# Casting in DMAs on Pool's queue in a sliding attention with an MLP behind it

## The chip, the cores and the metric

The kernel runs on one core of a Trainium2 chip. The metric is the device time of one execution in microseconds (us). The median of five runs before the change is 326.3 us (325.08 to 328.28).

A core has TensorE (PE, matrix products into PSUM), VectorE (DVE), ScalarE (ACT), GpSimd (Pool) and SyncE (SP). Each works through its own queue of instructions in order and waits for others only by semaphores. SP, ACT and Pool can issue DMA transfers; all of them run on the same 16 DMA engines.

## The reference

There are 8 batches, 8 heads, 576 positions and a head dimension of 64; q, k, v are fp32.

```python
scores = q @ k.T / sqrt(64)
mask_plain = (rel >= 0) & (rel < 32)                        # heads 0..3
mask_dil   = (rel >= 0) & (rel < 128) & (rel % 4 == 0)      # heads 4..7
attn = softmax(where(mask, scores, -1e9))
x = (attn @ v), heads side by side: 4608 tokens x 512
h = x @ w_in                        # 512 x 2048
out = maximum(0.01 * h, h) @ w_out  # 2048 x 512, fp32
```

## The kernel before, in words

Everything is computed on fp16 operands with fp32 sums. A **group** n (0 to 15) is four heads of one batch: n = 2 b for the plain heads and 2 b + 1 for the dilated heads of batch b. A **unit** u = 3 n + s is a third of a group's queries. The MLP goes over 13 chunks of tokens (CHUNKS, L20) for its first product and over 36 blocks of 128 tokens for its second.

The order of all work is written out in one string, PROGRAM (L26 to L72), whose words are issued one after the other (L360 to L396). Each engine's queue is the order of its own instructions in this list; where two words use different engines, their order in the list means little. The words:

- lq:n:p loads q and k of a group, one pair of heads (p = 0 or 1) or both (b). load_qk, L138, on SP. For groups 0 to 4 (n < NPE = 5) a partition holds 9 whole rows; for later groups a transfer has rows of 64 fp32, 256 bytes.
- lv:n loads v (load_v, L155, on SP): plain groups in 96 x 24 rows of 256 bytes, dilated groups in two transfers with rows of 1,024 bytes. Both go to a fp32 staging tile vf.
- lw:i:g loads a quarter of w_in (i = 0) or w_out (i = 1), 1 MB, on SP, into one of three staging tiles (L316).
- cq, cv, cw cast what was loaded to fp16 (L170, L183, L325), on the engine named by a letter: V VectorE, P Pool, A ScalarE. cv also copies v's last 32 partitions of each tile to partitions 0 to 31 of the next, as the window reaches back over a tile's edge.
- B:n:p transposes q and k of one pair on TensorE (pe_transpose, L202, 36 matmuls on 64 x 64), the two copies out of PSUM on the engines named. Groups 5 to 15 are transposed by DMAs instead (T, L197).
- S:u computes the scores of a unit and their exponential on ScalarE (L241). With b the mask is added first by a pair of matmuls from the tile bias; with m it is multiplied in later by M:u on VectorE (L264), from the tile mask.
- D:u sums the exponentials and multiplies with v on TensorE (L273), then takes the reciprocal, either on VectorE (r, one RECIPROCAL) or on ScalarE (l, an Ln and an Exp), and VectorE multiplies into xT, the MLP's input.
- I:c:j is a step of the first MLP product (L334, four matmuls and a ScalarE activation), O:t:g a quarter of a block of the second (L343); the last quarter is followed by a copy and a store on ScalarE's queue.
- Z:n are n filler matmuls on a tile of zeros (wp, L392), mask and band build the mask tiles on Pool (L102).

Two staging tiles hold q, two hold k, one each holds v of the plain and of the dilated heads; transposed q, k and fp16 v exist three times (NB = 3). The first MLP step, I:0:0, stands on TensorE behind 35 fillers, 6 B, 8 S and 6 D steps.

Of the kernel before, what the change touches and what calls it, by code (L numbers as in the profile page):

```python
# [9 lines left out]
FP16 = mybir.dt.float16  # L10
# [4 lines left out]
PAD = 128  # L15
B, H, S, D = 8, 8, 576, 64
DM = H * D
# [4 lines left out]
GRING = 1152  # L22
NEG = -30000.0
# [3 lines left out]
Z:3 lq:1:1 Z:8 lq:0:1 Z:2 cq:0:q:V:1 cq:1:k:A:1 Z:1 lq:0:0 lq:1:0 cq:1:q:P:1 lv:1:b Z:3 cq:0:k:A:1  # L27
B:1:1:VV Z:5 cq:0:q:V:0 Z:1 B:0:1:AA cq:1:k:P:0 Z:2 cq:1:q:V:0 Z:2 S:4:b B:1:0:VA lv:0:b lq:2:b
S:1:b lw:0:0 Z:1 cv:1:V:b cq:0:k:P:0 lq:3:b B:0:0:AA lw:0:1 S:3:b D:4:rp S:0:b D:3:lp cq:2:q:V:b Z:3
S:2:b Z:1 cv:0:P:b lw:0:2 D:0:lp cq:2:k:P:b D:1:l S:5:b B:2:1:AV B:2:0:VA cq:3:k:V:b Z:2 D:2:lp  # L30
cw:0:0:P lw:0:3 lv:2:b Z:1 cq:3:q:P:b S:7:m D:5:l mask S:6:m cw:0:1:V lw:1:0 I:0:0 I:0:1 M:7
B:3:0:AA S:8:m B:3:1:AV I:0:2 I:0:3 S:9:b I:0:4 cw:0:2:V I:0:5 I:0:6 M:6 I:0:7 S:11:m M:8 I:0:8
I:0:9 I:0:10 cw:0:3:V lw:1:1 I:0:11 I:0:12 I:0:13 cv:2:P:b cw:1:0:V I:0:14 I:0:15 cw:1:1:P lw:1:2
I:1:0 I:1:1 I:1:2 I:1:3 I:1:4 cw:1:2:P I:1:5 I:1:6 D:6:lp M:11 D:8:lp D:7:r S:10:m O:0:0 I:1:7 I:1:8
I:1:9 I:1:10 I:1:11 I:1:12 M:10 I:1:13 lv:3:b lw:1:3 O:1:0 O:0:1 O:1:1 cv:3:V:b I:1:14 lq:4:b O:2:0
O:2:1 cq:4:q:P:b cw:1:3:V lv:4:b lq:5:b I:1:15 cq:4:k:P:b O:0:2 D:11:l O:1:2 lq:6:b O:0:3 cq:6:q:P:b
D:10:l O:1:3 O:2:2 B:4:0:AV D:9:l B:4:1:VV S:12:m cq:5:q:V:b cq:5:k:V:b T:5 O:2:3 O:3:0 I:2:0 I:2:1
I:2:2 I:2:3 I:2:4 I:2:5 I:2:6 I:2:7 S:14:m I:2:8 I:2:9 I:2:10 I:2:11 cv:4:A:b cq:6:k:V:b O:3:1
I:2:12 lv:5:b T:6 M:14 O:3:2 I:2:13 M:12 lq:7:b O:3:3 I:2:14 lv:6:b cv:5:P:b I:2:15 I:3:0 I:3:1
I:3:2 O:4:0 I:3:3 I:3:4 S:13:m I:3:5 I:3:6 O:4:1 I:3:7 I:3:8 I:3:9 M:13 I:3:10 I:3:11 I:3:12 I:3:13  # L40
S:15:m D:12:r D:13:lp O:5:0 cq:7:q:P:b M:15 O:4:2 I:3:14 S:16:m M:16 cq:7:k:P:b T:7 lv:7:b lq:8:b
lq:9:b D:14:l O:5:1 O:4:3 S:17:m D:16:lp D:15:l I:3:15 cv:7:P:b M:17 O:5:2 O:6:0 O:6:1 I:4:0 O:5:3
I:4:1 S:19:m O:6:2 O:7:0 O:7:1 O:6:3 O:7:2 I:4:2 I:4:3 D:17:l S:20:m cq:9:k:P:b O:8:0 I:4:4 S:18:m
I:4:5 M:20 O:8:1 I:4:6 O:7:3 O:8:2 S:21:m I:4:7 cv:6:V:b I:4:8 M:18 M:19 D:20:lp S:22:m M:21 D:18:r
I:4:9 I:4:10 O:8:3 I:4:11 I:4:12 I:4:13 M:22 cq:8:k:V:b D:19:lp S:23:m D:22:lp D:21:l I:4:14 I:4:15
O:9:0 O:10:0 I:5:0 O:9:1 O:9:2 cq:8:q:V:b T:8 lv:8:b O:9:3 I:5:1 I:5:2 O:11:0 O:10:1 I:5:3 O:11:1
I:5:4 O:10:2 I:5:5 I:5:6 M:23 O:10:3 cq:9:q:P:b T:9 lq:10:b lq:11:b lv:9:b I:5:7 I:5:8 S:25:m D:23:l
I:5:9 O:11:2 I:5:10 I:5:11 I:5:12 I:5:13 I:5:14 M:25 I:5:15 I:6:0 I:6:1 O:12:0 I:6:2 O:12:1 S:26:m
O:11:3 I:6:3 I:6:4 I:6:5 cv:8:V:b I:6:6 S:28:m O:12:2 O:12:3 S:24:m cq:10:q:P:b I:6:7 I:6:8 I:6:9
O:13:0 cq:11:q:A:b I:6:10 I:6:11 O:13:1 M:28 S:27:m cq:11:k:P:b D:25:r I:6:12 I:6:13 cq:10:k:A:b  # L50
T:10 lv:10:b I:6:14 O:13:2 cv:9:P:b lv:11:b T:11 lq:12:b lq:13:b I:6:15 O:14:0 O:13:3 O:14:1 M:24
O:15:0 D:28:l S:29:m M:27 O:14:2 O:14:3 O:16:0 cq:12:k:P:b O:15:1 D:27:l D:24:lp S:30:m O:16:1
O:15:2 O:15:3 I:7:0 I:7:1 I:7:2 I:7:3 I:7:4 M:29 I:7:5 I:7:6 cv:10:P:b O:16:2 cq:12:q:P:b T:12
lv:12:b lq:15:b M:26 O:16:3 O:17:0 M:30 S:33:m D:29:lp D:26:l cv:11:V:b lv:13:b S:34:m M:33 I:7:7
O:17:1 I:7:8 I:7:9 I:7:10 I:7:11 M:34 I:7:12 I:7:13 I:7:14 D:33:r S:32:m cq:13:q:A:b O:17:2 D:34:lp
S:31:m O:17:3 M:31 I:7:15 O:18:0 O:18:1 D:30:lp D:31:l S:35:m M:35 O:18:2 O:19:0 O:18:3 I:8:0 I:8:1
I:8:2 I:8:3 I:8:4 cq:13:k:P:b T:13 lq:14:b S:38:m I:8:5 I:8:6 I:8:7 I:8:8 I:8:9 O:19:1 I:8:10 I:8:11
I:8:12 O:19:2 I:8:13 I:8:14 I:8:15 M:32 O:20:0 S:36:m M:38 D:35:rp D:32:l S:37:m O:19:3 O:20:1
O:20:2 cv:12:V:b cv:13:P:b M:37 O:21:0 O:20:3 O:22:0 cq:14:q:V:b cq:15:k:A:b M:36 O:21:1 O:22:1
I:9:0 I:9:1 D:38:l S:40:m O:21:2 I:9:2 M:40 O:21:3 I:9:3 cq:15:q:P:b T:15 lv:14:b I:9:4 I:9:5 I:9:6  # L60
D:37:l D:40:rp S:39:m O:22:2 I:9:7 S:41:m D:36:l I:9:8 O:22:3 O:23:0 I:9:9 O:23:1 cq:14:k:P:b T:14
lv:15:b I:9:10 O:23:2 M:39 I:9:11 O:23:3 D:39:l S:47:m I:9:12 I:9:13 I:9:14 I:9:15 M:41 I:10:0
I:10:1 O:24:0 O:24:1 M:47 I:10:2 S:46:m I:10:3 O:24:2 I:10:4 O:25:0 S:45:m cv:15:V:b D:41:l D:47:lp
S:42:m O:25:1 I:10:5 cv:14:V:b O:25:2 I:10:6 M:42 M:46 O:24:3 I:10:7 I:10:8 M:45 I:10:9 S:43:m
D:45:lp D:46:l O:26:0 M:43 I:10:10 O:25:3 I:10:11 I:10:12 S:44:m D:43:r D:42:lp I:10:13 O:26:1
I:10:14 I:10:15 O:26:2 O:26:3 I:11:0 I:11:1 I:11:2 O:27:0 I:11:3 I:11:4 I:11:5 I:11:6 M:44 O:27:1
O:27:2 O:27:3 D:44:lp I:11:7 I:11:8 O:28:0 I:11:9 I:11:10 I:11:11 O:29:0 I:11:12 O:28:1 I:11:13
O:29:1 O:28:2 I:11:14 I:11:15 O:29:2 O:28:3 I:12:0 I:12:1 I:12:2 I:12:3 O:30:0 O:30:1 O:29:3 I:12:4
O:30:2 O:31:0 O:30:3 I:12:5 I:12:6 I:12:7 I:12:8 I:12:9 I:12:10 O:32:0 O:31:1 I:12:11 I:12:12 O:31:2
I:12:13 O:31:3 O:32:1 I:12:14 I:12:15 O:33:0 O:32:2 O:34:0 O:32:3 O:33:1 O:34:1 O:35:0 O:33:2 O:34:2  # L70
O:33:3 O:35:1 O:34:3 O:35:2 O:35:3
# [4 lines left out]
def kernel(ctx: ExitStack, tc: tile.TileContext, q, k, v, w_in, w_out, out):  # L76
# [25 lines left out]
    def band(t, one, other):  # L102
# [7 lines left out]
    band(bias, 0.0, NEG)  # L110
# [5 lines left out]
    NB = 3  # L116
# [6 lines left out]
    vf = [cst.tile([128, 24, D], FP32, name="vf0"), cst.tile([128, 32, D], FP32, name="vf1")]  # L123
    nc.vector.memset(vf[1].rearrange("p (h a r) d -> p h a (r d)", a=2, r=4)[64:128, :, 1, :], 0.0)
    nc.scalar.copy(out=vf[0][0:32].rearrange("p (a t) d -> p a (t d)", a=3),
                   in_=warm[0:32].unsqueeze(1).to_broadcast([32, 3, 512]))
    for t in kT:
        nc.vector.memset(t[:, 0:PAD], 0.0)
        nc.vector.memset(t[:, S:PAD + S], 0.0)
    nc.vector.memset(vf[1][0:32], 0.0)  # L130
# [7 lines left out]
    def load_qk(n, pairs=(0, 1)):  # L138
        b, kind = divmod(n, 2)
        base = (b * H + 4 * kind) * S * D  # L140
        for nm, x in (("q", q), ("k", k)):
            if (n, nm) not in qkf:
                qkf[n, nm] = stg.tile([128, 24, D], FP32, tag=nm + "f", name=nm + "f")
            t = qkf[n, nm]
            if n >= NPE:
                nc.sync.dma_start(t[0:96], rows_ap(x, base, [[D, 96], [96 * D, 24], [1, D]]))
            elif len(pairs) == 2:
                nc.sync.dma_start(t[:, 0:18, :].rearrange("p (a t) d -> p a (t d)", a=2),
                                  rows_ap(x, base, [[9 * D, 128], [2 * S * D, 2], [1, 9 * D]]))
            else:  # L150
                p = pairs[0]
                nc.sync.dma_start(t[:, 9 * p:9 * p + 9, :].rearrange("p t d -> p (t d)"),
                                  rows_ap(x, base + 2 * S * D * p, [[9 * D, 128], [1, 9 * D]]))

    def load_v(n, pairs=(0, 1)):  # L155
        b, kind = divmod(n, 2)
        base = (b * H + 4 * kind) * S * D
        p0, p1 = pairs[0], pairs[-1] + 1
        if kind == 0:
            nc.sync.dma_start(vf[0][32:128, 12 * p0:12 * p1, :],  # L160
                              rows_ap(v, base + 1152 * D * p0, [[D, 96], [96 * D, 12 * (p1 - p0)], [1, D]]))
        else:
            t4 = vf[1].rearrange("p (h a r) d -> p h a (r d)", a=2, r=4)
            for a, i0, w in ((0, 0, 96), (1, 96, 48)):
                nc.sync.dma_start(t4[32:32 + w, 2 * p0:2 * p1, a, :],
                                  rows_ap(v, base + (1152 * p0 + 4 * i0) * D,
                                          [[4 * D, w], [S * D, 2 * (p1 - p0)], [1, 4 * D]]))


    def cast_qk(n, nm, eng, pairs=(0, 1)):  # L170
        if (n, nm) not in qkh:
            qkh[n, nm] = att.tile([128, 24 * D], FP16, tag=nm + "h", name=nm + "h")
        t, f = qkh[n, nm], qkf[n, nm]
        for p in pairs:
# [3 lines left out]
            else:  # L178
                eng(out=t[0:96, 12 * D * p:12 * D * p + 12 * D].rearrange(  # L179
                        "p (t h d) -> p h t d", t=6, h=2),  # L180
                    in_=f[0:96, 12 * p:12 * p + 12, :].rearrange("p (h t) d -> p h t d", h=2))

    def cast_v(n, eng, pairs=(0, 1)):  # L183
        t, f = vh[n % NB], vf[n % 2]
        p0, p1 = pairs[0], pairs[-1] + 1
        if n % 2 == 0:
# [240 lines left out]
```

The softmax here doesn't subtract the row's maximum and nothing guards it: scores larger than these inputs give would overflow.

## Time and profile before

| | |
|---|---|
| median of five runs | 326.3 us |
| profiled execution | 327.01 us, span 325.3 us |
| busy: TensorE / VectorE / ScalarE / Pool | 316.7 / 126.5 / 203.1 / 63.3 us |
| matmuls of the MLP, first and second product | 139.0 and 137.3 us |
| filler matmuls (wp) | 12.2 us |
| weight casts: 5 on VectorE, 3 on Pool | 6.8 and 5.7 us |
| read from / written to HBM | 36.70 / 9.44 MB |

The busy rows are sums over the span; the engines overlap, so they don't add up. The granted TensorE clock is full throughout (0.998 in the mean).

### The profile page before, as it was taken

The page shows a single profiled execution, that of the slowest core. Times are in us where ns is not written, and L with a number is a line of the kernel's source. Part 1 is how long each engine was busy: PE and PEld are TensorE (multiplying, and loading weights), DVE is VectorE, ACT ScalarE, POOL GpSimd, SP SyncE. Part 2 cuts the span into 40 slices and gives each one's busy share as a digit, 9 for nine tenths or more (in the row PEclk, how much of TensorE's full clock was granted, in tenths as well). Part 3 has the DMA queues.
Part 4 walks back from the last instruction along what each step waited for, and adds up shares of the span by engine and source line. Part 5 has one row for each costly group of instructions (what it writes and reads, how often), then busy time and mean ns, then how long its engine had stood idle before and what let it go on. Part 6 is the DMA issues. An engine that isn't in the chain of part 4 may idle for free.

```text
span 325.3 us, 6683 instructions
## 1 busy us (share of the span) xinstructions
PE 316.7 (97%) x2809; PEld 186.4 (57%) x2809; DVE 126.5 (39%) x173; ACT 203.1 (62%) x395; POOL 63.3 (19%) x66
## 2 busy tenths in 40 slices
PE   8979999999999999999999999999999999999995
PEld 2546676566755565565546556655665555555542
DVE  4598538560440783040413482076521670000000
ACT  4479883778765683566837787657764774543412
POOL 3273344025230600024000910062000000000000
PEclk9999999999999999999999999999999999999999
DMA  7999898979969105995099899609610000001012
GB/s 241 270 400 378 287 334 241 289 200 206 213 179 270 54 32 121 253 272 104 3 230 266 193 224 267 144 32 197 164 63 1 34 34 32 32 34 64 4 62 97
DMA packets 111198, 53.06 MB, mean 163 GB/s; under 512 B 96832, under 2 KB 101440, under 8 KB 110656
## 3 DMA queue, kind: packets, MB, share of 16 engines
q1 hardware_dynamic: 105984, 43.20, 53.9%
q10 hardware_dynamic: 5184, 9.44, 7.9%
q8 instruction: 22, 0.36, 0.5%
q14 instruction: 8, 0.07, 0.1%
HBM read 36.70 MB, written 9.44 MB: 142 GB/s over the span
## 4 chain that ended last, share of the span: by engine, by line
PE 93%; DVE 3%; ACT 2%; issue 1%; DVEq 0%
PE op L349 39%; PE hp L339 38%; PE sps L258 5%; PE wp L392 3%; PE den L284 3%; PE o L292 2%; PE tp L209 2%; ACT gt L341 1%; DVE rec L300 1%; DVE vh L195 1%; ACT er L261 0%; ACT ln L297 0%; DVE vh L192 0%; DVE qh L176 0%; ACT rec L298 0%
## 5 line engine op out<-in xcount | busy, mean ns | idle before, releaser
L339 PE MATMUL hp<-xT,w 128*128 128x384 f16 (+1 forms) x832 | 139.0, 315 | 0.7 <-DVE xT L309 0.7
L349 PE MATMUL op<-w,gt 128*128 128x512 f16 x576 | 137.3, 380 | 0.0
L341 ACT ACTIVATE gt<-hp 128x384 f16<-128x384 f32 (+1 forms) x208 | 93.5, 465 | 58.3 <-PE hp L339 56.1
L339 PEld LDWEIGHTS <-w 128*128 128x128 f16 x832 | 89.3, 114 | 43.7 <-DVE xT L309 1.2
L349 PEld LDWEIGHTS <-gt 128*128 128x128 f16 x576 | 54.6, 98 | 57.2 <-issue 0.7
L309 DVE TENSOR_TENSOR xT<-o,rec 128x384 f16<-128x384 f32 (+1 forms) x64 | 33.6, 553 | 95.8 <-ACT rec L298 94.3
L353 ACT COPY ob<-op 128x512 f32<-128x512 f32 x36 | 21.0, 584 | 36.9 <-PE op L349 36.8
L261 ACT ACTIVATE er<-sps 128x768 f16<-128x768 f32 (+1 forms) x48 | 38.6, 804 | 8.7 <-PE sps L258 7.5
L268 DVE TENSOR_TENSOR em<-er,mask 128x768 f16<-128x768 f16 (+1 forms) x41 | 25.2, 637 | 26.4 <-ACT er L261 26.0
L300 DVE RECIPROCAL rec<-den 128x384 f32<-128x384 f32 x9 | 23.0, 2552 | 20.2 <-PE den L284 20.2
L258 PE MATMUL sps<-qT,kT 64*128 64x96 f16 (+1 forms) x448 | 22.9, 229 | 0.6 <-ACT er L261 0.5
L297 ACT ACTIVATE ln<-den 128x384 f32<-128x384 f32 x39 | 18.9, 485 | 5.2 <-PE den L284 3.9
L179 POOL CAST kh<-kf 96x768 f16<-96x768 f32 x12 | 12.8, 1096 | 47.6 <-ACT gt L341 27.7
L258 PEld LDWEIGHTS <-kT 64*128 64x128 f16 (+1 forms) x448 | 15.2, 121 | 11.1 <-issue 9.4
L298 ACT ACTIVATE rec<-ln 128x384 f32<-128x384 f32 x39 | 20.4, 523 | 1.2
L179 POOL CAST qh<-qf 96x768 f16<-96x768 f32 x12 | 11.6, 994 | 36.4 <-DMA out_dram<-ob 26.5
L292 PEld LDWEIGHTS <-vh 128*64 128x64 f16 (+1 forms) x448 | 15.4, 110 | 2.4
L192 POOL CAST vh<-vf 128x2048 f16<-128x2048 f32 x4 | 7.6, 1892 | 41.7 <-PE o L292 25.6
L292 PE MATMUL o<-em,vh 128*64 128x96 f16 (+1 forms) x384 | 14.3, 201 | 0.0
L284 PE MATMUL den<-em,ones 128*64 128x384 f16 (+1 forms) x82 | 14.2, 343 | 0.0
L392 PE MATMUL wp<-xT 128*128 128x512 f16 x35 | 12.2, 458 | 1.7 <-DVE xT L114 1.3
L284 PEld LDWEIGHTS <-ones 128*64 128x64 f16 (+1 forms) x96 | 5.3, 107 | 7.8 <-issue 6.7
(55 smaller groups left out, 130.6 us busy)
## 6 DMA issues: line engine op xcount, KB each, us to landing
out_dram<-ob ACTq DMA_DIRECT2D x36, 256.0 KB, 2.1
qf<-in_q_dram SPq DMA_DIRECT2D x14, 576.0 KB, 7.3
kf<-in_k_dram SPq DMA_DIRECT2D x14, 576.0 KB, 7.2
vf<-in_v_dram SPq DMA_DIRECT2D x8, 576.0 KB, 6.2
wf<-in_moe_w_in_dram SPq DMA_DIRECT2D x4, 1024.0 KB, 11.4
wf<-in_moe_w_out_dram SPq DMA_DIRECT2D x4, 1024.0 KB, 8.8
vf<-in_v_dram SPq DMA_DIRECT2D x8, 384.0 KB, 6.2
vf<-in_v_dram SPq DMA_DIRECT2D x8, 192.0 KB, 5.2
```

The lines of the kernel that those rows point to most:

```text
L179: eng(out=t[0:96, 12 * D * p:12 * D * p + 12 * D].rearrange("p (t h d) -> p h t d", t=6, h=2), in_=f[0:96, 12 * p:12 * p + 12, :].rearrang ...
L258: nc.tensor.matmul(sps[0:kp, hh, w * x:w * x + w], ka, qa, start=not pe_mask, stop=not pe_mask or x == len(tiles) - 1)
L261: nc.scalar.activation(out=er[0:kp], in_=sps[0:kp, :, 0:384], func=AF.Exp, scale=SCALE)
L268: nc.vector.tensor_tensor(out=em[0:kp].rearrange("p h (t c) -> p h t c", c=w), in0=er[0:kp].rearrange("p h (t c) -> p h t c", c=w), in1=ba ...
L284: nc.tensor.matmul(den[64 * hh:64 * hh + 64, 0:384], ones[0:kp], em[0:kp, hh, :], start=True, stop=True)
L292: nc.tensor.matmul(o[64 * hh:64 * hh + 64, w * x:w * x + w], vt[0:kp, sl, :], em[0:kp, hh, w * x:w * x + w], start=True, stop=True)
L300: nc.vector.reciprocal(out=rec, in_=den[:, 0:384])
L309: nc.vector.tensor_tensor(out=out_x, in0=ins[0], in1=ins[1], op=ALU.mult)
L339: nc.tensor.matmul(hp[:, 0:w], w1[j // 4][:, i, j % 4::4], xT[:, i, x0:x0 + w], start=(i == 0), stop=(i == 3))
L341: nc.scalar.activation(out=gt[:, j, g0:g0 + w], in_=hp[:, 0:w], func=AF.Prelu, alpha=0.01)
L349: nc.tensor.matmul(op, gt[:, j, g0:g0 + 128], w2[g][:, j % 4, :], start=(j == 0), stop=(j == 15))
L392: nc.tensor.matmul(wp, warm[:, 0:128], warm, start=True, stop=True)
```

## The change

Weights, v, and q, k of groups 2 to 4 are no longer loaded as fp32 by SP and cast by an engine. Pool's queue issues transfers from fp32 in HBM straight into fp16 tiles. q and k of groups 0 and 1 are still loaded by SP in pairs and cast by engines, and so are q and k of groups 5 to 15. A new word gq loads q and k of a group in half precision. cw is gone; cv is now only the copy to partitions 0 to 31, from fp16. The staging tiles of v and of the weights are gone, and with them the zeros written to them; instead the parts of vh that no transfer fills are set to zero. Transposed q, k and fp16 v exist four times (NB = 4), fp16 q and k also four times (QHB = 4). The bias tile is built at a place in the list, behind the first load.

The list is a new one throughout. Fillers: 37 instead of 35. Score steps with bias matmuls: 4 instead of 7, so mask products: 44 instead of 41. Reciprocals on VectorE: 14 instead of 9. Ahead of I:0:0 stand 37 fillers, 6 B, 7 S and 6 D steps.

```diff
+lq:0:0 Z:2 bias lq:0:1 lq:1:0 lq:1:1 lv:0:b Z:4 cq:0:q:P:0 cq:0:k:V:0 Z:9 lv:1:b B:0:0:AA cq:0:q:P:1
+cq:0:k:V:1 Z:2 gq:3:b B:0:1:VA cq:1:k:P:0 S:0:b cq:1:q:P:0 Z:7 cq:1:q:V:1 lw:0:0 B:1:0:VV cq:1:k:A:1
+S:1:m Z:3 B:1:1:AA Z:1 S:2:b Z:1 mask M:1 Z:1 cv:0:V:b D:0:rp S:3:b lw:0:1 D:1:lp gq:2:b cv:1:P:b
+Z:2 S:5:m D:3:lp Z:2 S:4:b lw:0:2 B:3:1:VA M:5 lw:0:3 B:3:0:VA lv:2:b Z:2 D:4:l D:2:lp D:5:lp Z:1
+gq:4:b S:11:m I:0:0 I:0:1 I:0:2 S:10:m lw:1:0 M:10 I:0:3 I:0:4 cv:2:P:b S:9:m I:0:5 B:2:1:AV I:0:6
...
-    NB = 3
+    NB = 4
...
+    for i in (1, 0, 3, 2):
+        nc.vector.memset(kT[i][:, 0:PAD], 0.0)
+        nc.vector.memset(kT[i][:, S:PAD + S], 0.0)
+        t = vh[i][0:32, 0:24:12, :] if i % 2 == 0 else vh[i][0:32].rearrange("p (h a r) d -> p h a (r d)", a=2, r=4)[:, :, 0, :]
+        nc.vector.memset(t, 0.0)
...
+    def load_half_qk(n, pairs):
+        for nm, x in (("q", q), ("k", k)):
+            t = half(n, nm)[:, 9 * D * pairs[0]:9 * D * pairs[-1] + 9 * D]
+            nc.gpsimd.dma_start(t.rearrange("p (a r) -> p a r", r=9 * D), qk_ap(x, n, pairs))
+
+    def load_v(n, pairs):
...
+        t = vh[n % NB]
         if kind == 0:
-            nc.sync.dma_start(vf[0][32:128, 12 * p0:12 * p1, :],
...
+            nc.gpsimd.dma_start(t[32:128, 12 * p0:12 * p1, :],
+                                rows_ap(v, base + 1152 * D * p0, [[D, 96], [96 * D, 12 * (p1 - p0)], [1, D]]))
+        else:
+            t4 = t.rearrange("p (h a r) d -> p h a (r d)", a=2, r=4)
             for a, i0, w in ((0, 0, 96), (1, 96, 48)):
...
+                nc.gpsimd.dma_start(t4[32:32 + w, 2 * p0:2 * p1, a, :],
...
+    def copy_v(n, eng, pairs):
+        t = vh[n % NB]
+        p0, p1 = pairs[0], pairs[-1] + 1
         if n % 2 == 0:
...
+            eng(out=t[0:32, 12 * p0 + 1:12 * p1, :], in_=t[96:128, 12 * p0:12 * p1 - 1, :])
+        else:
+            t4 = t.rearrange("p (h a r) d -> p h a (r d)", a=2, r=4)[:, 2 * p0:2 * p1]
+            eng(out=t4[0:32, :, 1, :], in_=t4[96:128, :, 0, :])
...
     def load_w(i, g):
-        t = stg.tile([128, 4, 512], FP32, tag="wf", bufs=WF, name="wf")
         if i == 0:
...
+            nc.gpsimd.dma_start(w1[g], rows_ap(w_in, 512 * g, [[DFF, 128], [128 * DFF, 4], [1, 512]]))
+        else:
+            nc.gpsimd.dma_start(w2[g].rearrange("p t c -> p (t c)"),
+                                rows_ap(w_out, 512 * g * DM, [[4 * DM, 128], [1, 4 * DM]]))
```

## The prediction

> **What bounds the kernel now.** I read the page's slices first, then the busy time by stretch, then the chain of work that ended last in order of time, then the order of time itself (VectorE, Pool and SP separately). The table of stretches says where time can be had at all. Its columns: stretch, length, busy time and instruction count of PE, its weight loads, VectorE, ScalarE and Pool, then granted clock, DMA share and GB/s.
>
> ```profile
> 10.00:15.00 5.00, 4.67 (x100) 2.56 (x97) 2.20 (x5) 2.52 (x4) 1.28 (x2) 1.00 1.05 224
> 15.00:20.00 5.00, 4.55 (x83) 2.53 (x83) 4.94 (x3) 4.04 (x7) 4.44 (x4) 1.00 1.02 378
> 20.00:25.00 5.00, 3.66 (x114) 2.79 (x115) 4.92 (x7) 4.24 (x8) 3.32 (x5) 1.00 1.05 406
> 30.00:60.00 30.00, 29.25 (x322) 19.65 (x316) 17.51 (x20) 20.28 (x46) 10.28 (x8) 1.00 0.97 288
> 60.00:320.00 260.00, 259.94 (x2060) 152.27 (x2058) 87.71 (x120) 162.22 (x319) 38.85 (x34) 1.00 0.55 131
> ```
>
> From 60 to 320 us TensorE is idle for 0.06 us, from 30 to 60 for 0.75 us. There the time is TensorE's own work, and no faster cast buys anything. Only the start has slack, and there VectorE is full from 15 to 25 us. The chain shows what TensorE waited for (start, length, what):
>
> ```profile
> 14.43 1.23 DVE vh L192
> 15.65 0.02 issue
> 15.68 1.83 DVE vh L195
> 17.51 2.48 DVE rec L300
> ...
> 21.55 0.65 DVE qh L176
> 22.20 1.25 issue
> 23.45 0.45 DVE qh L176
> 23.90 0.04 issue
> 23.95 1.32 PE tp L209 x72
> ```
>
> The reader is to see VectorE's casts of v and q of the first batches on the chain, and that the first MLP matmul (hp, L339) comes only at 28.21 us. I call that moment I0. Before it TensorE does its attention steps and 35 filler matmuls (wp); the first 17 fillers take 7.03 us, the rest about 0.27 us each by the chain's pieces. After I0 it is 293.5 us to the last matmul's end, then the last copy and store. So the question is what the change does to I0.
>
> **The change part by part.**
>
> *TensorE's own work.* After I0 there are 41 score steps instead of 40 (+0.35 us by an 8-matmul step at 0.34 to 0.35), and the one score step with a bias matmul pair left there goes (-0.33 of TensorE by the L246 group's 328 ns mean, two per pair partly side by side). MLP steps, value steps and transposes are as many. The sum after I0 is zero within 0.1 us. Five more reciprocals (14 for 9, 2.55 us each, 12.8 us) and three more mask products (0.63 each) go to VectorE, and five Ln and Exp pairs (0.49 + 0.52) leave ScalarE. I cost both at nothing: after 60 us VectorE is busy 88 of 260 us and ScalarE 162 of 260. If that cover failed at a value step, TensorE would wait up to the 1.5 us by which a reciprocal is longer than a pair, once for each.
>
> *TensorE's path to I0 without any wait.* 15 fillers ahead of the first transpose: 1.32 + 15 x 0.414 = 7.5 us. Then 17 fillers (4.6), four transpose steps (0.69 each, 2.8), five score steps (three with bias at 0.7, one 0.35, one 0.71: 3.2) and two value steps (0.33 each) bring it to D:3, at 18.7 us. From D:3 to I0: three value steps beside it, S:4 and S:11, two transpose steps and five fillers, 5.55 us. So I0 is 24.3 us at the earliest. By the same sum the kernel before could have had 24.9 and has 28.2: it loses 3.4 us to the VectorE waits above.
>
> *What leaves VectorE.* Of those, the cast of v (1.22) goes, and the second v copy works on fp16 that is there already (some 1.1, the L195 group's median on VectorE, in place of 1.83); the casts of q and k of groups 2 and 3 (2.34, and 1.15 at 26.1 us) go, since DMAs write fp16. So 4.3 us of the 10.5 that VectorE works from 14.4 to 25 us are gone; five weight casts of 1.36 us go later (hidden already). I add up VectorE's new list from D:0 at 16.5 us: a reciprocal 2.54, products and one mask 2.7, two transpose copies 1.5, a product 0.7: done at 24.0, just ahead of I0. So VectorE no longer sets I0, but it has no slack.
>
> *What comes to Pool's queue.* Pool now issues every weight, value and half-precision q, k transfer, in line with its casts, and each instruction behind an issue waits for it. Up to the v shift copy that D:3 needs, Pool's list is: start and bias, done at 3.14 as now; lv:0 (1 transfer), cast, lv:1 (2), cast, gq:3 (2), two casts, lw:0:0 (1), mask, lw:0:1 (1), gq:2 (2), cv:1. That is 9 issues, four casts at 0.65 (L176 on Pool, 0.64 to 0.66 when alone), the mask 2.15 (four instructions), and the shift copy 1.03 (L195 on Pool). Without the issues Pool is there at 8.9 us. TensorE wants D:3 at 18.7. **So nine issues may take 9.8 us, 1.09 each, before TensorE waits, and 13.7 us, 1.52 each, before I0 is as late as now.**
>
> No issue on Pool is in this trace. The nearest row is SP's, for a load of the same kind:
>
> ```profile
> 2.68 0.43 SPq L152 DMA_DIRECT2D qf<-in_q_dram  x1
> ...
> 6.73 0.31 SPq L160 DMA_DIRECT2D vf<-in_v_dram  x1
> ```
>
> That is the low bound, 0.4 us (3.9 us for nine), on a queue with hardware behind it. The Trainium skill, "SBUF — State Buffer" (SBUF: two separate sides), speaks against the change: software on GpSimd writes the descriptors of a transfer on Pool's queue, through the port pair that VectorE's two-port copies lock, so that a transfer of 0.62 us becomes 3.1 us beside one. The trace shows the lock between the two engines on casts: VectorE's two q casts take 0.82 us with Pool idle and 2.34 us while Pool casts weights.
>
> ```profile
> 10.13 0.82 DVE L176 CAST qh<-qf 128x576 f16<-128x576 f32 x2
> ...
> 21.32 1.89 POOL L326 CAST w<-wf 128x2048 f16<-128x2048 f32 x1 [1.12 <-DMA wf<-in_moe_w_in_dram]
> ...
> 21.55 2.34 DVE L176 CAST qh<-qf 128x576 f16<-128x576 f32 x2
> ```
>
> By the page's free figure nine issues are 5.6 us and Pool is early; by its blocked figure they are 27.9 us and I0 is 14.5 + 27.9 = 42.4. I stand near the free end: in the first 25 us VectorE's long items are now a reciprocal and PSUM copies, and its fp32 casts from SBUF fall from seven to three (0.41 to 0.46 each) and one fp16 copy. "DMA: Bandwidth & Descriptors" (Specifications, and Anatomy of one DMA) gives about 1 us to the first byte on this path, and calls the cost of more descriptors small; no run here shows either. I take 1.0 for each, and 1 more for lv:0, whose 2,304 rows of 256 bytes are the most: 10 us, Pool at 18.9, TensorE's 18.7. The two meet.
>
> *Transfers.* The DMA engines are full from 5 to 60 us. Now SP's eight first loads share them with lv:0 and lv:1, which stood behind them on SP. Between 4 us and the last q, k landing (about 11.2 now) some 0.6 MB comes in between, 1.7 us at 350 GB/s; fillers (Z:2, Z:7) cover about half. I take 0.8 us on the path. The bytes read are the same, half as many are written; I cost the cast inside the transfer at nothing, with the bound in the rivals. Behind I0, lw:0:2 and lw:0:3 are issued at about 20 and 21 us and wanted at I:0:8 and I:0:12, some 8 us after I0. SP's queue loses 8 weight and 24 value issues, and nobody waits for it more than before.
>
> *Sum.* I0 = 24.3 + 0.2 (Pool) + 0.8 (landing) = 25.3, so 2.9 us earlier. The profiled execution took 327.01 us (span 325.3 and 1.7 around it): 324.1. Against the median of the five runs, 326.3: **323.4 us**, -0.9%. 0.5% (1.6 us) is about what a measurement of this kernel can tell from no change.
>
> **The rivals.**
>
> *Pool's queue becomes the bound (slower).* One mechanism: D:3 waits for cv:1, which stands behind nine issues on Pool. For it: Pool's list up to there is serial, a load issued early (gq:3) stands ahead of casts that TensorE wants, and software per row may be like Pool's software per element (its selects take 0.53 us for 384 elements, 1.4 ns; at that rate the 4,928 rows are 6.8 us on top of nine times 1.0). Then I0 = 14.5 + 15.8 = 30.3. At 2.0 us each, which the DMA page gives as the fixed part of a whole transfer, I0 is 32.5, 4.3 later: 330.6; at 30.3 it is 328.4. At the blocked figure: 340.5. It decides from 1.52 us an issue. Against it: 1.09 each is free. Chance 0.28, about 330 (between the two).
>
> *Transfers that cast run slower (slower).* If the 5.6 MB that are cast ahead of B:2 count double, the engines must pass 13.6 MB, 36 us at 378 GB/s, and TensorE, wanting B:2 about 5 us after I0 (30 us), waits 6 to 8 us: 330. For it: full DMA engines, and 256-byte rows that become 128-byte ones. Against it: nothing in the trace shows casts in a DMA. Chance 0.10.
>
> *Another wait takes the place (same).* VectorE's list ends at 24.0 with no slack, and scores share one PSUM tile with ScalarE's exponentials (0.81 us each). With 2 us of that I0 is at 27.3: 325.4. Chance 0.12.
>
> *The forecast.* I0 at 24.3 to 26.5: 322.4 to 324.6. Chance 0.50.
>
> **How the numbers follow.** The likeliest case gives 323.4, its own range is 322 to 324.7. The two slower cases hold 0.38; the far end of Pool's (beyond 2.4 us an issue, 334) is about 0.12 of it and left out, and 0.06 below 321.7 (TensorE's path beaten, if fillers warm up sooner). So 321.7 to 334. Faster by over 0.5%: 0.50; within: 0.12; slower: 0.38.
>
> **What would show it.** Right: the first hp matmul at 24.3 to 26.5 us; no vh or qh piece of VectorE on the chain at 14 to 24 us; issues on Pool near 1 us; cv:1 done by 19 us; 60 to 320 us still without idle. Wrong: Pool issues of 1.5 us or more, lv:0 above 4 us, and TensorE's idle in the first 30 us ended by Pool's casts or copies; or q, k, v landings far behind their issues (slow casting transfers); or new idle behind 60 us, which would say that transfers on Pool's queue come too late in the steady part, a thing that I cost at nothing.

## The result and the profile after

| | before | after |
|---|---|---|
| median (runs) | 325.72 us (80) | 324.70 us (43) |
| ratio of the times, 95% interval | | 0.9969 (0.9957 to 0.9982) |
| profiled execution, span | 327.01, 325.3 us | 325.25, 323.5 us |
| I0, first matmul hp | 28.21 us | 24.43 us |
| last op matmul (second product) starts | 321.30 us | 319.58 us |
| from I0 to that | 293.09 us | 295.15 us |

The kernel is 0.31% faster, 1.0 us, where 2.9 us were forecast. The start gained 3.78 us, more than forecast; after I0 TensorE took 2.06 us longer, where the forecast had no change. One matmul of before shows its I0, and one a wait that comes back below (start, length, then the idle time before it and what ended it):

```profile
28.21 1.49 PE L339 MATMUL hp<-xT,w 128*128 128x384 f16 x8
...
48.59 1.84 PE L339 MATMUL hp<-xT,w 128*128 128x192 f16 x20 [0.74 <-DVE xT L309]
```

The chain of waits of the changed kernel, in order of time (start, length, what):

```profile
3.15 1.25 POOL vh L169
...
5.01 10.19 DMA vh<-in_v_dram
...
15.26 1.03 POOL vh L198
16.29 0.69 POOL w L320
16.98 19.83 DMA w<-in_moe_w_in_dram
...
36.86 4.44 PE hp L334 x36
...
59.81 7.15 DMA out_dram<-ob
...
67.04 0.59 ACT ob L348
```

VectorE's casts of v, q and k are gone from the chain. In their place stands a transfer of weights that Pool issued at 16.98 us and that landed 19.83 us later, and after it a store that took 7.15 us. The order of time on TensorE shows what the first did (start, length, then the idle time before it and what ended it):

```profile
24.43 2.14 PE L334 MATMUL hp<-xT,w 128*128 128x384 f16 x12
...
33.53 0.84 PE L334 MATMUL hp<-xT,w 128*128 128x384 f16 x4 [0.72 <-DMA w<-in_moe_w_in_dram]
```

This is I:0:8, the first step on w_in's third quarter; from matmul start to matmul start TensorE loses 0.88 us there and 0.30 at I:0:12, near 36.6 us, for the fourth. At 66.8 and 68.2 us it loses 0.68 and 0.26 more: ScalarE, which empties hp, stands behind the store's buffer (ob). The table of stretches has the same idle time (PE is the second column of figures; the DMA share, the last but one, adds up the times of packets and can pass 1):

```profile
15.00:20.00 5.00, 5.00 (x71) 2.82 (x70) 3.58 (x3) 3.65 (x7) 3.79 (x5) 1.00 1.22 199
20.00:25.00 5.00, 4.94 (x139) 3.72 (x134) 3.92 (x7) 4.49 (x10) 1.40 (x2) 1.00 1.20 194
30.00:60.00 30.00, 29.12 (x383) 19.22 (x378) 10.98 (x16) 20.70 (x47) 10.96 (x14) 1.00 1.37 181
60.00:320.00 260.00, 259.35 (x1971) 150.31 (x1968) 84.49 (x117) 150.31 (x299) 40.09 (x44) 1.00 0.62 117
```

From 20 to 25 us VectorE is down from 4.92 to 3.92 and TensorE up from 3.66 to 4.94; from 60 us on TensorE now idles 0.65 us, where it had 0.06. Pool's own order of time has the issues that the forecast could only bound:

```profile
3.10 1.30 POOL L169 DMA_DIRECT2D vh<-in_v_dram  x1
...
7.49 0.73 POOL L161 DMA_DIRECT2D qh<-in_q_dram  x1
...
10.29 0.75 POOL L320 DMA_DIRECT2D w<-in_moe_w_in_dram  x1
...
15.26 1.03 POOL L198 COPY vh<-vh 32x1024 f16<-32x1024 f16 x1
```

They cost 0.6 to 1.3 us, nine of them 7.0 us, and cv:1, the last line, is done at 16.29. And SP's order of time has what the forecast overlooked:

```profile
7.57 0.33 SPq L152 DMA_DIRECT2D qf<-in_q_dram  x1
8.10 8.96 SPq L152 DMA_DIRECT2D kf<-in_k_dram  x1
```

This is lq:5, the load of q and k of group 5. Before, it stood on SP behind weights and values:

```profile
47.16 8.27 SPq L146 DMA_DIRECT2D qf<-in_q_dram  x1
55.47 1.90 SPq L146 DMA_DIRECT2D kf<-in_k_dram  x1
```

With those on Pool's queue nothing stands ahead of it but the free buffers, and it goes out 40 us early, ahead of every weight. Its last byte landed at 38.48 us; the w_in quarters, issued from 10.3 to 17 us, took 15.4 us in the median to land (11.4 before, where they were plain loads on SP).

### The profile page after: what moved, and what is told of

The parts are those of the page before. It is cut to its first block, busy times and chain, and to the rows that moved or that the text cites. A ratio compares the mean times of both kernels' runs of the same rounds, so it can differ in the third digit from the quotient of the medians.

```text
span 323.5 us, 6641 instructions
## 1 busy us (share of the span) xinstructions
PE 316.9 (98%) x2805; PEld 185.3 (57%) x2805; DVE 111.9 (35%) x166; ACT 191.6 (59%) x379; POOL 69.9 (22%) x92
## 4 chain that ended last, share of the span: by engine, by line
PE 85%; DMA 11%; POOL 2%; ACT 1%; issue 0%; ACTq 0%; POOLq 0%
PE op L344 38%; PE hp L334 36%; DMA w<-in_moe_w_in_dram 6%; PE sps L261 5%; PE den L287 3%; DMA vh<-in_v_dram 3%; PE o L295 2%; DMA out_dram<-ob 2%; ACT ob L348 1%; PE tp L212 0%; POOL vh L169 0%; POOL vh L198 0%; POOL w L320 0%; POOL qh L183 0%; POOL bias L106 0%
## 5 line engine op out<-in xcount | busy, mean ns | idle before, releaser
L334 PE MATMUL hp<-xT,w 128*128 128x384 f16 (+1 forms) x832 | 141.3, 315 | 1.5 <-DMA w<-in_moe_w_in_dram 0.7
L303 DVE RECIPROCAL rec<-den 128x384 f32<-128x384 f32 x14 | 35.8, 2556 | 36.0 <-PE den L287 36.0
L186 POOL CAST kh<-kf 96x768 f16<-96x768 f32 x16 | 13.1, 842 | 103.9 <-DMA kf<-in_k_dram 78.6
L300 ACT ACTIVATE ln<-den 128x384 f32<-128x384 f32 x34 | 16.6, 488 | 8.7 <-PE den L287 8.1
L301 ACT ACTIVATE rec<-ln 128x384 f32<-128x384 f32 x34 | 17.8, 524 | 1.1
L295 PE MATMUL o<-em,vh 128*64 128x96 f16 (+1 forms) x416 | 15.4, 201 | 0.0
L287 PE MATMUL den<-em,ones 128*64 128x384 f16 (+1 forms) x88 | 15.4, 346 | 0.0
L174 POOL DMA_DIRECT2D vh<-in_v_dram x16 | 10.0, 627 | 19.2 <-PE o L295 19.2
L195 POOL COPY vh<-vh 32x1472 f16<-32x1472 f16 x5 | 7.4, 1472 | 28.4 <-DMA vh<-in_v_dram 28.3
## 6 DMA issues: line engine op xcount, KB each, us to landing
w<-in_moe_w_in_dram POOLq DMA_DIRECT2D x4, 512.0 KB, 15.4
```

The lines of the kernel that those rows point to most:

```text
L287: nc.tensor.matmul(den[64 * hh:64 * hh + 64, 0:384], ones[0:kp], em[0:kp, hh, :], start=True, stop=True)
L295: nc.tensor.matmul(o[64 * hh:64 * hh + 64, w * x:w * x + w], vt[0:kp, sl, :], em[0:kp, hh, w * x:w * x + w], start=True, stop=True)
L301: nc.scalar.activation(out=rec, in_=ln, func=AF.Exp, scale=-1.0)
L303: nc.vector.reciprocal(out=rec, in_=den[:, 0:384])
L334: nc.tensor.matmul(hp[:, 0:w], w1[j // 4][:, i, j % 4::4], xT[:, i, x0:x0 + w], start=(i == 0), stop=(i == 3))
```

## The experiments

**Theory 1**: Pool's transfers and lq:5 share the same engines, and lq:5, released early, makes w_in late. **Theory 2**: the cast inside a transfer makes transfers late. **Theory 3**: the time given back after I0 lies elsewhere, at the store for one.

**Holding lq:5 back.** One word in the list and a copy of 128 bytes on SP, which waits for the eighth MLP step:

```diff
-... M:9 I:0:7 I:0:8 S:7:m ...
+... M:9 I:0:7 gate:7 I:0:8 S:7:m ...
+        elif f == "gate":
+            nc.sync.dma_start(scr, gt[0:1, int(a[0]), 0:64])
```

> The changed kernel, and SP's load of q, k of group 5 held back by a 128-byte copy on SP that waits for the eighth MLP step. Nothing else on SP is held, for nothing else stands between. Theory 1 (shared engines: that load, which no longer stands behind weights and values, runs from 7.6 us among the transfers on Pool's queue and makes the quarters of w_in late): the third and fourth quarter of w_in land some 3 to 5 us earlier (33.5 and 36.8 us in the changed kernel), the two waits of TensorE for them (0.9 and 0.3 us) are gone, and the time falls by about 1.2 us against the changed kernel, 0.7% under the kernel before. Theory 2 (the cast inside a transfer is what makes them late): the landings move by less than 1.5 us and the time by less than 0.4 us. Theory 3 (the given-back time lies elsewhere): the landings move, the time doesn't.

Measured: 323.42 us, ratio to before 0.9943 (0.9917 to 0.9969). I0 is at 24.32, w_in's quarters land 10.1 us after their issue in the median (15.4), the last two 6.0 and 6.7 us earlier than in the changed kernel. SP's order of time, the rows of w_in's transfers in the changed kernel and here (count, size of one, median us from issue to landing), and TensorE's order of time where the wait was:

```profile
33.77 0.85 SPq L152 DMA_DIRECT2D qf<-in_q_dram  x1
```

```profile
w<-in_moe_w_in_dram POOLq DMA_DIRECT2D x4, 512.0 KB, 15.4
w<-in_moe_w_in_dram POOLq DMA_DIRECT2D x4, 512.0 KB, 10.1
```

```profile
31.65 1.49 PE L335 MATMUL hp<-xT,w 128*128 128x384 f16 x8
33.07 0.34 PE L261 MATMUL sps<-qT,kT 64*128 64x96 f16 x8
33.35 4.82 PE L335 MATMUL hp<-xT,w 128*128 128x384 f16 x29
```

I:0:8 runs in one piece with I:0:7, and no step is late. From I0 to the last op it is 292.8 us, where the forecast had 293.1 unchanged. The median is 1.4 us under the next kernel's, the changed one but for its output tiles, which ran beside this one. The mechanism of theory 1 is shown: only SP's queue from lq:5 on was held back.

**A longer store chain (ob in four buffers).**

```diff
-            ob = moe.tile([128, DM], FP32, tag="ob", bufs=2, name="ob")
+            ob = moe.tile([128, DM], FP32, tag="ob", bufs=4, name="ob")
```

> The changed kernel with four output tiles in place of two, so that ScalarE's copy of a finished block doesn't wait for a store to land. In the changed kernel a copy waits 3.2 us for a store that took 7.15 us, and TensorE loses 0.7 and 0.3 us behind it near 67 us. If that wait is a term of what is given back: the time falls by 0.7 to 1.0 us against the changed kernel. If the store's delay only moves TensorE's waits to the next slot (input tiles of the same PSUM pool): less than 0.3 us.

Measured: 324.82 us, ratio 0.9972 (0.9947 to 0.9996). The wait at 67 us isn't in its profile, and the time isn't distinguishable from the changed kernel's. Both together:

> The load of group 5 held back as before, and four output tiles in place of two. With the load held back the stores near 58 to 65 us still take 5 us, but the profile shows no wait of TensorE there. If the output tiles are a term of their own: 0.5 us or more under the held-back kernel's 323.4. If their wait was only the engines' backlog: within 0.3 us of it.

Measured: 324.12 us, ratio 0.9936 (0.9915 to 0.9957); nothing beyond the gate alone. Against the changed kernel beside it (324.79, next) the two together bring 0.7 us.

**The changed kernel once more**, beside these:

> The changed kernel itself once more, as the control for the runs beside it: 0.3% under the kernel before, about 324.7 us.

Measured: 324.79 us, ratio 0.995 (0.993 to 0.997). Its profile separates the two waits. TensorE's order of time:

```profile
32.73 0.84 PE L334 MATMUL hp<-xT,w 128*128 128x384 f16 x4 [0.62 <-DMA w<-in_moe_w_in_dram]
```

The wait for weights is there again (0.79 and 0.30 us from start to start), the one at the store isn't: from I0 to the last op it is 294.1 us, 1.0 more than before. So 1.1 us of the 2.06 come each time, and 0.94 us, at the store, came in one of two profiled executions. With four ob buffers it brought nothing that the medians show.

**Transfers alone.** A kernel with no attention and no MLP (its output is zeros) loads four w_in quarters, four w_out quarters, q rows and v rows, first plain on SP, then cast on Pool's queue. The stages of weights and q are issued when the one before has landed; from the v stages on, later loads already go out while earlier ones land.

> Not the reference's computation: only transfers, one kind after the other with a join between, and zeros written out. Four loads each of w_in quarters (2,048-byte rows), w_out quarters (8,192), q of a group (2,304) and v of a plain group (256), plain on SP and then casting on Pool's queue; then w_in casting on Pool's queue beside v rows on SP, and w_in plain on ScalarE's queue beside v rows on SP. Theory 2 (the cast has its price in the engines): casting takes 10 to 15% longer on the large rows and about 1.8 times as long on 256-byte rows, as the packets' own times in the changed kernel say (96 for 84 ns, 32 for 18 ns). Theory 1 needs no such price: equal times within 5%, and a casting w_in beside v rows stretched by the rows' own share, as much as a plain one.

The order of time of SP and Pool (a stage lasts until the next line's start; the SP copies end the cast stages):

```profile
0.74 2.41 SPq L122 DMA_DIRECT2D F<-in_moe_w_in_dram  x4
14.14 3.10 POOL L126 DMA_DIRECT2D G<-in_moe_w_in_dram  x4
27.48 0.59 SPq L135 DMA_DIRECT2D sc<-fh  x1
...
64.30 2.83 POOL L126 DMA_DIRECT2D G<-in_q_dram  x4 [0.35 <-issue]
75.01 0.50 SPq L135 DMA_DIRECT2D sc<-fh  x1
...
98.51 4.68 POOL L126 DMA_DIRECT2D G<-in_v_dram  x4 [0.40 <-issue]
...
106.03 0.76 POOL L144 DMA_DIRECT2D G<-in_moe_w_in_dram  x1 [2.85 <-DVE fh L134]
...
111.25 0.16 DVE L134 COPY fh<-G 1x4 f16<-1x4 f16 x1 [1.71 <-DMA G<-in_v_dram]
...
111.99 15.73 SPq L145 DMA_DIRECT2D R<-in_v_dram  x4
...
133.17 0.14 DVE L147 COPY fl<-R 1x1 f32<-1x1 f32 x1 [2.29 <-DMA R<-in_v_dram]
```

From first issue to last landing w_in takes 13.2 us plain and 13.1 cast, w_out 12.6 and 12.4, v in rows of 256 bytes 13.4 (in a later stage, where it stood alone) and 12.7 (with a plain w_in quarter still landing beside it until 103.4 us), q in rows of 2,304 bytes 8.9 and 10.4. Each was measured once. A cast costs a transfer nothing for three of four shapes, 17% for one; as a reason for w_in's late landing, theory 2 falls.

The last four lines are w_in cast on Pool's queue beside v plain on SP. Until 111.2 us the v casts of the stage before are still landing, so the two are alone from there on: 22.0 us to the last landing, for four v loads and most of four w_in quarters, which take 13.4 and 13.1 us alone. **Two queues have one set of engines between them: together the loads take far longer than either alone.** Who pays is another matter. In this stage w_in's landings went from 2.5 us apart to 3.3 and 3.5, while the v loads took 21.2 us instead of 13.4. In the changed kernel it was w_in that paid: lq:5's two loads of the same rows are, by 13.4 / 4 = 3.35 us each, an estimated 6.7 us, and 6.7 us is what the gate gave back to the last quarter. Why it fell on w_in there stays open.

**Weights loaded plainly** on SP and cast by engines in the new list (three staging tiles; one ln buffer, and fp16 q, k three times, to make room):

```diff
-            nc.gpsimd.dma_start(w1[g], ...)
+            nc.sync.dma_start(t, ...)
...
+        elif f == "cw":
+            cast_w(int(a[0]), int(a[1]), ENG[a[2]])
```

> The weights' part undone in the changed kernel: weights by plain loads on SP into three fp32 tiles, one cast on Pool and seven on VectorE at places of my choice in the list, the fp16 q, k tiles 3 instead of 4 for room. SP's queue has the weights ahead of group 5 again. Theory 1 and 2 both have the weights land earlier than in the changed kernel (w_in's last quarter by 32 us or earlier) and no wait of TensorE for them; by theory 1 the time is 1 to 1.5 us under the changed kernel as long as the casts are hidden. If instead taking the casts off the engines is what brought the start's 3.8 us, the first MLP step comes 1 us or more later than 24.4 us and the time is at or over the kernel before.

Measured: 332.78 us, ratio 1.0226 (1.0196 to 1.0256), I0 at 32.37. By the last clause of the expectation this would speak for the casts. The chain shows another cause:

```profile
3.10 17.79 DMA vh<-in_v_dram
...
20.99 0.55 DVE vh L195
```

SP issues three weight quarters from 4.8 us on, and they share the engines with Pool's lv:0, which lands at 20.89 us, not 13.53. This looks like theory 1 with other partners. To test that, the same kernel with an SP copy that waits for group 1's v ahead of the first weight load:

```diff
-... cq:1:q:V:1 lw:0:0 B:1:0:VV ...
+... cq:1:q:V:1 vgate lw:0:0 B:1:0:VV ...
+        elif f == "vgate":
+            nc.sync.dma_start(scr, vh[1][32:33, 4, :])
```

> The kernel with plain weight loads on SP and engine casts (332.8 us), and in addition a copy of 128 bytes on SP's queue ahead of the first weight load that waits until Pool's load of v of group 1 has landed. Theory 1: v of group 0 lands at 13 to 14 us again instead of 20.9, the first MLP matmul is back from 32.4 to 24.5 to 26, and the time is 323.5 to 326. Theory 2 or another (the weights' own way to fp16 is what counts): the first MLP matmul stays above 28.5 and the time above 328.

Measured: 328.86 us, ratio 1.0062 (1.0029 to 1.0096). lv:0 lands at 12.40 and I0 is back at 25.67, as expected. The time isn't as expected: Pool's weight cast, which I had put into Pool's queue ahead of lv:2 and gq:4, waits for its weights until 23.6 us. The chain:

```profile
14.61 8.99 DMA wf<-in_moe_w_in_dram
...
25.56 1.20 POOL vh L169
26.76 0.69 POOL qh L161
27.45 19.78 DMA kh<-in_k_dram
...
47.27 1.06 PE tp L212 x54
```

gq:4 goes out 6.5 us later than in the changed kernel, and its k lands at 47.22, beside w_out. This is the price of a wait on a queue that issues loads.

**Parts in the old list.** Only v on Pool's queue (group 12's v is loaded over group 8's before its last use, so group 8's attention is computed from other values):

```diff
-    NB = 3
+    NB = 4
-            nc.sync.dma_start(vf[0][32:128, 12 * p0:12 * p1, :],
+            nc.gpsimd.dma_start(t[32:128, 12 * p0:12 * p1, :],
```

> The kernel before with one part of the change alone: v cast by DMAs on Pool's queue (with the copy to partitions 0 to 31, and four tiles of transposed q, k and of v in place of three), all other casts and the list as before. If VectorE's v and q casts at 14.4 to 24 us set the first MLP step: the cast of 1.2 us goes, the copy shortens by 1 us, and the step comes at 26 to 27 us instead of 28.2; time 0.3 to 0.6% under the kernel before. If the new list, with its order of fillers and transposes, is what brought the start's gain, the step stays within 0.7 us of 28.2.

Measured: 347.33 us, ratio 1.0619 (1.0552 to 1.0685). I0 is at 42.66, outside both cases: lv:0, issued at 11.76 us behind a cast on Pool, took 20.7 us beside SP's weights, and TensorE stood idle for 11.2 us until it landed. So this run doesn't show what VectorE's casts of v alone are worth.

Only the weights, and weights with v (the load of group 12's v moved behind its buffer's last reader), each with the words cw taken out of the list:

```diff
-            nc.sync.dma_start(t, rows_ap(w_in, ...
+            nc.gpsimd.dma_start(w1[g], rows_ap(w_in, ...
```

> The kernel before in its own list, with only the weights turned to fp16 by transfers on Pool's queue; v, q and k stay plain loads and engine casts. Theory 1 (what counts is which transfers run side by side): SP's loads of v, q, k keep their order among themselves, so v lands as before (within 1.5 us) and only the casts of q that ran beside Pool's weight cast get shorter: the first MLP matmul at 26.5 to 28, 324.5 to 326. Theory 3 (it is the casts of v, q and k leaving VectorE that brought the start): the first MLP matmul within 0.5 us of 28.2 and 325.5 to 327. If weights on a second queue hold v back as in the kernel with plain weights: the first MLP matmul above 29 and over 327.

> The kernel before in its own list, with weights and v by transfers on Pool's queue (four v tiles in place of three, the load of group 12's v moved behind its tile's last reader); q and k of all groups stay plain loads and engine casts. Theory 1: weights and v stand in one queue again, so v isn't held back by weights as it was with v alone on Pool's queue (where v of the first groups landed at 32 us); it lands by 15 us, and with 3 us of casts gone from VectorE the first MLP matmul comes at 25.5 to 27, 323.5 to 325.5. If transfers on Pool's queue suffer whatever runs beside them, v lands after 18 us and the first MLP matmul comes after 29, over 327.

Measured: weights alone 327.47 us, ratio 1.0032 (0.9998 to 1.0065), I0 at 28.84; with v 330.60 us, ratio 1.0137 (1.0089 to 1.0185), I0 at 30.32. Neither gains anything. Both lie outside what theory 1 led me to expect, and the second has the numbers of the other case (v after 18 us, over 327). But its reason is another: a load of v takes no longer here than in the changed kernel (9.7 and 10.4 us), it is issued late. With weights alone lq:2's k took 10.17 us (5.41 before) beside the weights on the other queue. With both, the chain reads:

```profile
11.08 0.60 POOL kh L172
11.68 9.68 DMA vh<-in_v_dram
...
21.53 1.41 POOL vh L183
```

Pool casts k of group 1, which landed at 11.03, and only then issues lv:0; in the changed kernel it goes out at 3.10.

**The new list alone**, all loads plain on SP, all casts by engines, three buffers:

```diff
-... cq:0:k:V:1 Z:2 gq:3:b B:0:1:VA ...
+... cq:0:k:V:1 Z:2 lq:3:b B:0:1:VA ...
-... lw:0:2 B:3:1:VA M:5 ...
+... lw:0:2 cq:3:q:P:b cq:3:k:V:b B:3:1:VA M:5 ...
```

> The new list alone: every transfer is a plain load on SP and every turn to fp16 an engine cast, as in the kernel before, but the words stand in the order of the changed kernel, with the casts of q, k of groups 2 to 4 put just ahead of their transposes and the weight casts where the kernel with plain weights had them (three buffers as before; four words moved back behind the last reader of their buffer). If the start's gain of 3.8 us comes from the list (which loads stand first, fewer bias matmuls), the first MLP matmul comes before 25.5 us and the time is 322 to 325. If it comes from the casts that leave VectorE and Pool (the prediction's reason), the first MLP matmul comes at 27 to 30 and the time is 325.5 to 329.

Measured: 341.54 us, ratio 1.0442 (1.04 to 1.0485), I0 at 31.72. Pool's weight cast stands ahead of group 3's q, and that was my placing. From I0 on it takes 305.1 us where before took 293.1; part of that is a wait of 4.3 us at 37.0, when TensorE needs a q that Pool has yet to cast. So this shows that the list with these casts doesn't bring the start, not what the list or the casts alone are worth.

**Gate, and three fillers fewer:**

```diff
-Z:2 S:5:m ... lv:2:b Z:2 D:4:l D:2:lp D:5:lp Z:1
+Z:2 S:5:m ... lv:2:b D:4:l D:2:lp D:5:lp
```

> The load of group 5 held back, and three of the 37 fillers left out (two ahead of D:4, one ahead of S:11). By the trace D:4 could run at 21.4 instead of 22.0 us, ScalarE's reciprocal and VectorE's product behind it free the first MLP step by 0.5 us. Expected: the first MLP step at 23.7 to 23.9 us instead of 24.3, and 0.4 to 0.6 us under the held-back kernel. If ScalarE's exponentials, not the fillers, set that end, the step stays at 24.3 and the time is the same.

Measured: 323.35 us, ratio 0.9911 (0.9875 to 0.9946), I0 at 23.88. This beats the kernel before, and it is the best version tried. Its interval is clear of the changed kernel's first one (0.9957 to 0.9982) and touches the second (0.993 to 0.997), with 1.4 us between the medians taken side by side. Against the gate alone its median is 0.07 us lower, and I0 was at 23.93 in one execution of the changed kernel with all its fillers; what leaving them out adds isn't settled.

## Why the prediction was half right

- **I0**, forecast 25.3 us, came at 24.43 and 23.93 in two profiled executions, and at 24.32 to 25.15 in the three that add the gate, four output tiles or both. "TensorE's path to I0 without any wait", 24.3, was about what the chip did; the 0.2 (Pool) and 0.8 (landing) added to it weren't needed. The last q, k of the first two groups landed at 11.49 us, 0.34 later than before.
- **Pool's queue**, forecast 10 us for nine issues and the limit 9.8, took 7.0 us. The bound from SP's row (3.9) was too low; one price for all was wrong too: the measured ones rise with the number of rows, 0.56 (w_out), 0.71 to 0.75 (q, k, w_in), 1.2 to 1.3 (plain v). The rival "Pool's queue becomes the bound" is out.
- **The lock** that the Trainium skill's "SBUF — State Buffer" (SBUF: two separate sides) sets against such issues hardly shows in the changed kernel ahead of I0, as the forecast supposed: lv:0 took 1.30 us with VectorE idle beside it, and the largest stretch is 0.84 us for an issue of 0.71 (q of group 2, beside a copy of VectorE's). It does show where VectorE casts weights (below).
- **"Transfers that cast run slower"** is out for weights and v by the transfers measured alone; for q and k it holds with 17%, far from the double count of that case.
- **VectorE's list** was no bound: nothing of it is on the chain.
- **The step that failed** is the end of "Transfers": "Behind I0, lw:0:2 and lw:0:3 are issued at about 20 and 21 us and wanted at I:0:8 and I:0:12, some 8 us after I0. SP's queue loses 8 weight and 24 value issues, and nobody waits for it more than before." It put the wait for w_in after I0 at nothing. The quarters were issued earlier than that, at 16.2 and 17.0, and TensorE was ready for them at 32.7 and 36.6, but they landed at 33.5 and 36.8. I asked who waits for SP's queue; the question was what SP's queue does once nothing stands ahead of it. lq:5 lost the weights and values ahead of it, started 40 us early, and made w_in's last quarter land 6.7 us later.
- **TensorE's own work**, "The sum after I0 is zero within 0.1 us", was off too, by less. Where no wait is left, the new list takes 292.8 to 293.1 us from I0 to the last op (the three kernels with the gate), the old one 292.3 (the two with weights on Pool's queue). It looked like zero because the profile of before held a wait of its own, 0.91 us from start to start at 47.6 us. Which steps make the new list 0.5 to 0.8 us longer wasn't tested.

In numbers: the wait for w_in was put at 0 and measured 1.2 and 1.1 us in the two profiled executions of the changed kernel; the wait at the store was 0.94 us in one of them. With lq:5 held back the wait for w_in is gone, from I0 on it takes 0.3 us less than before (292.8 against 293.1), and the medians are 323.4 and 324.1 us, against 323.4 forecast.

That doesn't account for all. In the profiles the changed kernel gains 1.8 and 3.3 us; between the medians 1.0. The one profiled execution of before, from which the sum was made, was itself 1.3 us over its kernel's median of 80 runs, whose times go from 323.7 to 330.0. The wait of 0.91 us isn't in the two old-list kernels above, so it may be most of the 1.3, and its start may have been a late one too; one profile can't tell, and that stays open. What also stays open is which part brings the start. Weights and v on Pool's queue without the list bring nothing, the list without the transfers (with my placing of casts) neither. With weights plain and held behind v, the start is 1.2 us later than in the changed kernel and 2.5 earlier than before; that points to v and q, k cast by transfers that go out early, in a list made for it, but no run has them without the new list.

## What to carry to other kernels

When loads move from one queue to another, the loads that stay lose what held them back: write down for each queue which transfer now goes out first, when, and beside which wanted one. The wanted one can pay for the whole of the other, as w_in's last quarter did here with 6.7 us. A load that nobody wants soon must be given something to wait for. And a queue that issues loads should hold no cast that waits for other loads.

## What the hardware showed beyond that

A VectorE cast of weights (128 x 2,048 fp32 to fp16) stretches an issue on Pool's queue. In the kernel with plain weights behind v, Pool's order of time:

```profile
26.75 0.71 POOL L161 DMA_DIRECT2D qh<-in_q_dram  x1
27.45 1.36 POOL L161 DMA_DIRECT2D kh<-in_k_dram  x1
...
49.92 1.94 POOL L169 DMA_DIRECT2D vh<-in_v_dram  x1
```

The second ran beside a cast from 27.44 to 28.66 us and ended 0.15 us after it, so an issue of 0.71 became 1.36. The third began beside a cast that ended at 51.06; an issue of 1.19 became 1.94. That cast took 1.94 us instead of 1.22 too, but Pool's copy of v (48.94 to 49.97 us) ran beside its first half, so what the issue did to it isn't shown. By the page the blocked engine waits until the other's instruction is over, which fits the second; the page's 3.1 us was not seen beside casts of 1.2 us. The changed kernel has no such casts left.

A long wait of TensorE cost more than its length. In the kernel with v alone on Pool's queue the granted clock was 0.50 from 25 to 40 us, during and after the wait of 11.2 us that ended at 32.5. With the new list alone the wait of 4.3 us ended at 41.3; the clock was 0.57 from 40 to 45 us, and four hp matmuls took 1.47 us there instead of 0.84. In the kernel before and in the changed one, where TensorE waits 1.3 us at most from 5 us on, it was 1.00 in every stretch up to 320 us.
